# Feed-forward units past the fourth summed in one PSUM bank, scaled there by ScalarE between second and third products, with the engines' lists searched anew

## The chip, the core and the metric

The kernel runs on one core of a Trainium2 chip. The metric is the device time of one execution in microseconds (us), as the median of several runs. Inside the core, TensorE (PE, with its weight loads shown apart as PEld), VectorE (DVE), ScalarE (ACT) and GpSimd (POOL) each work through an own list of instructions in order, and wait for one another by semaphores. SyncE (SP) issues transfers. Matrix products land in PSUM, which has eight banks of 512 fp32 columns here; GpSimd has no operand in PSUM in this kernel.

## The reference

The program is an attention block with inducing points, followed by a gated feed-forward block over all tokens, in fp32. B = 4 batches of N = 12416 tokens with C = 128 channels, m = 32 inducing rows, d_ff = 1536.

```python
def mab(q, kv):
    s = scale * (q @ kv.transpose(0, 2, 1))
    s = s - s.max(-1, keepdims=True)
    a = np.exp(s)
    a /= a.sum(-1, keepdims=True) + 1e-09
    return a @ kv
h = mab(I, x)
x = mab(x, h)                      # then, on all 49664 tokens:
rms = np.sqrt(np.mean(x * x, axis=-1, keepdims=True) + 1e-06)
xn = x / rms * rms_g
g = xn @ w_gate
silu = g * (1.0 / (1.0 + np.exp(-g)))
val = xn @ w_val
out = silu * val @ w_out
```

## The kernel before

**Units and blocks.** The tokens of a batch are cut into 25 units: 20 of 512 tokens, 4 of 480 and 1 of 256, so 100 units in all (`flat`). A unit has 12 blocks (`blocks`, index j), one for each 128 of the 1536 inner columns. The 32 attention weights of a token stand for it (`a`, four stacked copies), and the gate and value weights are folded with the batch's inducing rows (`stacks`), so that a block's gate (`gate`, L720) and value (`value`, L748) are one TensorE pass each. ScalarE takes the silu (`silu`, L730), VectorE multiplies by the value (`times_value`, L762).

**Three sorts.** What follows for a block is set by its letter in the table `sorts`:

- P: `project_plain` multiplies the fp32 factor by the fp32 output weight `wo` (L818, two records in the trace for each block).
- S: the factor is left in its PSUM bank, ScalarE makes its high part (`high`, L775), VectorE the low part (`low`, L781), both as fp32r.
- D: the factor lies in SBUF, ScalarE makes the high part (L772), GpSimd the low part (`low_of_u`, L788), ScalarE scales the high part down (`high_down`, L794).

S and D then run three fp32r passes: `project_two` (L806 and L807, the first and second products), then GpSimd adds the two parts in place (`add_in_place`, L826), and `project_third` (L818) multiplies that sum by a third weight.

**Two banks a unit.** First and second products of a unit are summed in the bank `one["ups"]`; third and plain products are summed in another, `one["acc"]`. The ups sum has to be scaled by 1 + 2^-12. Four steps finish a unit: `scale_up` (E, ScalarE, L850) takes ups out of PSUM into an SBUF tile `o`, scaled and reordered; `finish` (F, VectorE, L859) adds acc to it; `turn_out` (T, VectorE, L865) transposes `o` in 32 x 32 blocks in place; `store` (O, SyncE, L880) sends it out. E needs all second products of the unit, F all third and plain ones.

**What sets the order.** There is no scheduler. The string `program` lists the steps by letter in the order in which they are issued, and each engine takes its own in that order; a dot takes the next small step of the attention of the next batch (`micros`, `taken`). Other strings give each step its resources: `banks` the PSUM bank of each product, `holders` one of 19 rooms of 512 columns for the factors (`room`), `outputs` the tile `o`, `picks` which of the waiting blocks a step takes (steps E, F, T, O take units in their order, without a pick). Rooms 0 to 8 are tiles of the pool `up`. The other ten are slices of three tiles of the first batch's x, which `rooms` opens once that batch's x has been used; the trace calls them xn.

Of the kernel before, what the change touches and what calls it, by code (L numbers as in the profile page):

```python
# [18 lines left out]
P = 128  # L19
# [4 lines left out]
def kernel(  # L24
# [40 lines left out]
    RING, HELD, SILU = 4, 9, 3  # L65
# [17 lines left out]
    psum = pool("psum", 1, space=PSUM)  # L83
    pall = psum.tile([P, 8, 512], F32, name="gv")
# [9 lines left out]
    def load_rows(b, s):  # L94

        n = per[s]
        t = xnat[b, s] = xnp.tile([P, 16 if b and n > 4 else n, C], F32, name=f"xn{s % 2 if b and n > 4 else s}")
# [592 lines left out]

    blocks, kinds = [], []
# [7 lines left out]
    def unit_of(b, u):  # L699
        if (b, u) not in at_unit:  # L700
            s, q = units[u]
            at_unit[b, u] = {"T": per2[s] * m, "a": moving.pop((b, u)), "left": NJ, "q": 0, "acc": None,
                             "k": sum(kind != "P" for kind, one in zip(kinds, blocks) if one[:2] == (b, u)), "o": None,
                             "ups": None}
# [92 lines left out]
    def project_two():  # L797
# [4 lines left out]
        if one["ups"] is None:  # L802
            one["ups"] = bank()
        to = one["ups"][:, 0:T]
# [6 lines left out]
    def project(n, lhsT, rhs, step2):  # L811
# [3 lines left out]
        if one["acc"] is None:  # L815
            one["acc"] = bank()
        to = one["acc"][:, 0:T]
        nc.tensor.matmul(to.rearrange("p (n h) -> p h n", h=2) if step2 else to, lhsT, rhs,  # L818
                         start=one["left"] == NJ, stop=one["left"] == 1)
# [18 lines left out]
    leaving = {name: 0 for name in "EFTO"}  # L838

    def next_unit(name):  # L840
        leaving[name] += 1
        return flat[leaving[name] - 1]

    def scale_up():
# [3 lines left out]
        T, o = one["T"], output(F32)  # L848
        one["o"] = o
# [11 lines left out]
    def turn_out():  # L861
        b, u = next_unit("T")
        one = unit_of(b, u)
        o, T = one["o"], one["T"]
# [393 lines left out]
    def seams():  # L1258
# [13 lines left out]
        5674130256741352764156216710562160121607267012750671527162067125701527061352701372301273016276370142374017436107  # L1272
        5461701375601735764301674317642376476324736426173214672670321071507125625625730261325620463042603435423046754672
        6571574124615247601207502765127520730717157312014520712054051402460524124361406470341720123014073145207145205162
        4076176230451603542360267402340264706402613067507602716510250673501637521352614563175416571674605740534715702545
        3457042563253265431275126142745265124560124607164701640316370347147057304132041201372013720317603270307256042750
        4756027457256347203174063021462176270675246510461307635063450634573460543604265230541265026504265026316241321643
        1064370613041320741327342735407234507234657403254130421502401325140275130732713621762170617301612506031041234610
        4621046513052135720175237120372130276215601670416415074560743514305436543215362160524062534217541646314735673157
        3561746147560274265462502530726546253601460362013460724104270371274205402507215724175061045614061306531405310463  # L1280
        5013674034130461204372104672503725074604365073047654304716046074107160721504712670235072130536725603505237062407
        2314760162062746015412574251346547516421541257642576072605210572153701357127034152342375276132436236724632174260
        7540152406524150621504361053606250125726507650216745012475627452743564527342654736024670261720742160726034704320
        1472014721542015430174301574231654215634251467354216352615236025301253012765320532154725347254712563174217637523
        0752370635767540372103120437204312072430730145703175601314341703641706327102751301341735407364103410543265123614
        2351425312634175725647256172010457015472134270321026701630513620712605763476237062046267210473623561561453612546
        3210523025043570145370641763120547163047305173501630763120750674561027475467045074507245626034013453165034150326
        4520132435743051217230723165016371043651306704754053640356435270342704175027517251427507164721453264534516342164
        5320164532405127451723407312403612753123512561726532756127032160342560324053246302542164321024052472014725041275
        4327031240370173104731643143072641362013562150613570615263174521621452643256416312654036254720764065205621562756  # L1290
        0461043103560401403507471054615042704627160734102374130415021704170527054761045260123646504615304673106351670515
        6725120513657106723017346123461762167341527647362746502364576215367425762156246276570647274635074067450367513541
        3657426517365127605360130232046352162146574051760415704761350735705327537210570673160752635725473427635274152645
        3273157425073215023576031706527106241065476140173546703573061362013651036013243162015714251640542016204310546154
        3103601765732053210642367412702173273407417520715231603573156743061471567051725417627452617425143610742642604276
        0124051264701256140
    """
    workers = """
        20120201201201020120122201201201201201211210210201020120110120120
    """  # L1300
    outputs = """
        10101010101010101010101010101010101010101010101010101010101010101010101010101010101010101010101010101010
    """
    holders = """
        abcdefghibcaedfghbicjkadelmfghnobcidepqarsfgbhidjkaeclmpnfoqrsgjhbidklaecpnfgdombrqsjihpagoecdfbknilmpghrqfsjlmc
        pkinobrsadqjhpkgfelmnoqcjrspbliadnmjkoqsglhrfejpaodnqbscriekjapmlnsqogkrbfpjhsaecokqrmdilnopgskmhqbcjrefolmnipqs
        ajdgchmkfepoirnbgqlsrpmckjfoqglnpsmibkohadprelsjmcgfnkbqolpiahdrjemsqfrcgbhnoiljepkqmrsdnloaqjifrcgpmsonblkqejrp
        hsgialnfqpojmkdsrlnqcpombeijsplqhfdagknromqepijchalskdgfbrmepqjnhgaifcokjpbrlqgeinosmdrlajpqhskmnrcfbloqmjidesag
        frklcjpqnosmhbdrlgiejkafdqpcbrmelonsfgcqjidpkhablroqenmfgicdjshaoedcinpqlgbjkhsdiorfbhgemnaqocspfjkrigbhdlmasncq
        pfedjorgbsnkclqmhefirjabposknlqemdrgibfhpoqscajnlmfhkrpecidjnbgqosljmafkdpnrqcoskihgbpefcadjlmrhosapndqkgehpjmin  # L1310
        obflrqdspkcmjnqholgaesbfkpdolhminqfjrskcpogmljdfnrqbpcaoskjhgiqmlpnefodqrmknlpcsmijknabolpshgjeidbfocgnkhqrplmjs
        oaifehgcnbdkpqclhrgfdesmjnrofkqilpgsrobkdjqlmhcnseljamrpqknfoiglspmcoqjkldhrsnpelabjmokqngircjfdhblsemqpnokjgamq
        rdlipejfmscpqonklhmgsaberjocpikmlpdsrhefqngobaljpikdmhcqsrleonfagbmpjreqolciknmpsqholfjgbakderichfsnmqopaljbrkcf
        moglhiaedbrjckqegdpsnlfrjiedkqmoaghcpsnrfblmikendagojlqhcfbmpiarsnlgckmfdhqbpoidejnaqkhipdgerbasohjlgmqienpfkrcs
        adhjnglmbpsqofekrjpidgscbljqnhepkafomgisqrnbplkcohjmfsrgkpaqbeoijdlsgnmqrfeokabpjnmlcgqhafdibeopgsrklnjcqmobkgln
        hsqdpriomajlkceshnpbofiarqsmndgejklobipnhcsgldefmraqchbjkopaslmnqirohjgdqbpmeknfsalrcidjfqokegplsdjmrknbsphcgljr
        mqasifnpeokljdhcgfrqmsolnpbekjromialsfnqpkgrjmondqlhscpnkrmbefiaojsqglkdphnmrclskoerigapjnrfbkdhlosqnmpkrsjelgpi
        acnhfjrmlpoqkdnsjbremgqkfjapdhnrifmlcesqjkbgophnrmjceoslpnadkqimofjgnbshdrlcminjoeafbkqdgpschmnjofrpdksblqamrige
        jnchpoblkqsfdagmjirnpohecqslkrpbmjdfnloqaskighmoeqcbsjrpnlagqmdikshofnejcabrlgqpdmkohirnbsldfaqjcpmkoriegsqlknjp
        ofdbshemrlqpncsgoaibklpmejshnqorkcjbplnfksqomjrdgapnqkoemicrlphjqbgnmorsfakjploqcsdnipebghorfcqksmlpjonradbcqfse  # L1320
# [240 lines left out]
```

## Time and profile before

| what | value |
| --- | --- |
| median of 3 runs | 1468.44 us (1467.72 to 1468.91) |
| the profiled execution, first to last instruction | 1467.1 us |
| mean granted TensorE clock | 0.999 |
| ScalarE busy | 1300.0 us, 89% |
| blocks of sort P, S, D | 371, 649, 180 |
| E, F, T, O steps | 100 each |
| moved by transfers | 116.02 MB, mean 79 GB/s |

The profile gives one execution, whose span is 1467.1 us. It lists each engine's busy time as the union of its records; records of one engine can overlap, so an engine's real pace is read from one start to the next. In the rows, the first name is the line of the kernel, then engine, operation, what is written and what is read.

### The profile page before, as it was taken

How to read it: one execution, taken by the hardware profiler on the slowest of the kernel's cores; microseconds unless marked ns; L12 is line 12 of the kernel's file. 1: busy time of each engine (PE TensorE's matmuls, PEld its weight loads, DVE VectorE, ACT ScalarE, POOL GpSimd, SP SyncE). 2: the span in 40 equal slices, each digit the busy share in tenths (PEclk: the TensorE clock that was granted, in tenths of full speed). 3: DMA queues.
4: the chain of work that ended last, by engine and by line, in shares of the span. 5: the costliest groups of instructions: out<-in, count | busy, mean ns of one | idle time of the engine just before them, and what ended most of it. 6: DMA issues, size and time to landing. Idle time of an engine off the chain costs nothing.

```text
span 1467.1 us, 25864 instructions
## 1 busy us (share of the span) xinstructions
PE 1460.2 (100%) x7293; PEld 1111.8 (76%) x7293; DVE 1423.3 (97%) x2476; ACT 1300.0 (89%) x2586; POOL 1353.0 (92%) x1193
## 2 busy tenths in 40 slices
PE   9999999999999999999999999999999999999998
PEld 7556777877777777786777778777778778788787
DVE  6999999999999999999999999999999999999998
ACT  6798899889988989988999899888998999899987
POOL 2578998999999999899999999799999999999998
PEclk9999999999999999999999999999999999999999
DMA  7656224445654222635554132355123111222121
GB/s 282 137 99 119 58 49 92 103 107 99 118 88 99 38 44 44 141 84 105 110 101 82 26 73 43 63 119 127 34 62 70 33 37 39 43 42 38 36 45 33
DMA packets 391904, 116.02 MB, mean 79 GB/s; under 512 B 365648, under 2 KB 371280, under 8 KB 389200
## 3 DMA queue, kind: packets, MB, share of 16 engines
q1 hardware_dynamic: 391168, 114.28, 37.7%
q8 instruction: 58, 0.95, 0.3%
q14 instruction: 86, 0.70, 0.2%
q10 hardware_dynamic: 592, 0.08, 0.0%
HBM read 53.95 MB, written 27.00 MB: 55 GB/s over the span
## 4 chain that ended last, share of the span: by engine, by line
PE 99%; DVE 0%; DMA 0%; ACT 0%; issue 0%; DVEq 0%
PE gv L818 33%; PE gv L720 17%; PE gv L748 17%; PE gv L806 12%; PE gv L807 12%; PE gv L327 3%; PE gv L380 1%; PE gv L945 1%; PE gv L574 1%; PE gv L989 0%; PE gv L468 0%; PE gv L158 0%; PE gv L490 0%; DMA ind<-in_inducing_dram 0%; PE gv L567 0%; PE gv L1099 0%
## 5 line engine op out<-in xcount | busy, mean ns | idle before, releaser
L730 ACT ACTIVATE silu<-gv 128x512 f32<-128x512 f32 (+2 forms) x1200 | 678.1, 591 | 89.4 <-PE gv L720 67.4
L826 POOL TENSOR_TENSOR xn<-xn,xn 128x512 fp32r<-128x512 f32 (+2 forms) x363 | 453.0, 1259 | 23.4 <-PE gv L807 14.5
L720 PE MATMUL gv<-a,sg 128*128 128x512 f32 (+2 forms) x1188 | 463.5, 415 | 0.1
L748 PE MATMUL gv<-a,sv 128*128 128x512 f32 (+2 forms) x1188 | 460.9, 415 | 0.0
L762 DVE TENSOR_TENSOR gv<-silu,gv 128x512 f32<-128x512 f32 (+2 forms) x649 | 427.1, 673 | 6.5 <-ACT silu L730 2.2
L775 ACT ACTIVATE xn<-gv 128x512 fp32r<-128x512 f32 (+2 forms) x602 | 353.1, 594 | 25.8 <-DVE gv L762 20.5
L818 PE MATMUL gv<-u,wo 128*128 128x512 f32 (+2 forms) x742 | 364.1, 576 | 0.0
L762 DVE TENSOR_TENSOR u<-silu,gv 128x512 f32<-128x512 f32 (+2 forms) x551 | 352.3, 654 | 7.8 <-PE gv L748 3.7
L826 POOL TENSOR_TENSOR u<-xn,u 128x512 fp32r<-128x512 f32 (+2 forms) x239 | 298.3, 1257 | 5.6 <-PE gv L807 4.1
L720 PEld LDWEIGHTS gv<-a,sg 128*128 128x128 f32 x1188 | 223.9, 189 | 86.8 <-issue 21.5
L748 PEld LDWEIGHTS gv<-a,sv 128*128 128x128 f32 x1188 | 223.8, 189 | 80.6 <-issue 23.0
L781 DVE SCALAR_TENSOR_TENSOR xn<-xn,gv 128x512 fp32r<-128x512 f32 (+2 forms) x410 | 268.9, 662 | 4.7 <-ACT xn L775 2.7
L826 POOL TENSOR_TENSOR xn<-xn 128x512 fp32r<-128x512 f32 (+2 forms) x170 | 211.4, 1250 | 11.4 <-PE gv L807 10.3
L806 PE MATMUL gv<-xn,xn 128*128 128x512 f32 (+2 forms) x450 | 177.4, 394 | 0.0
L818 PEld LDWEIGHTS gv<-u,wo 128*128 128x128 f32 x742 | 139.1, 190 | 29.7 <-issue 14.2
L788 POOL TENSOR_TENSOR xn<-u,xn 128x512 fp32r<-128x512 f32 (+2 forms) x123 | 152.3, 1243 | 6.8 <-ACT xn L772 5.5
L781 DVE SCALAR_TENSOR_TENSOR u<-xn,gv 128x512 fp32r<-128x512 f32 (+2 forms) x192 | 125.8, 660 | 1.2 <-ACT xn L775 0.9
L818 PE MATMUL gv<-xn,xn 128*128 128x512 f32 (+2 forms) x299 | 117.3, 398 | 0.0
L806 PE MATMUL gv<-xn,more 128*128 128x512 f32 (+2 forms) x302 | 116.0, 385 | 0.0
L794 ACT ACTIVATE xn<-xn 128x512 fp32r<-128x512 f32 (+2 forms) x170 | 105.6, 623 | 8.2 <-POOL xn L788 4.0
L807 PE MATMUL gv<-xn,xn 128*128 128x512 f32 (+2 forms) x299 | 111.6, 373 | 0.0
L772 ACT ACTIVATE xn<-u 128x512 fp32r<-128x512 f32 (+2 forms) x170 | 104.9, 621 | 3.9 <-DVE u L762 1.7
(233 smaller groups left out, 2049.8 us busy)
## 6 DMA issues: line engine op xcount, KB each, us to landing
out_dram<-o SPq DMA_DIRECT2D x320, 64.0 KB, 2.0
xT<-in_x_dram SPq DMA_DIRECT2D x60, 256.0 KB, 4.1
xn<-in_x_dram SPq DMA_DIRECT2D x60, 256.0 KB, 5.0
a<-hi SPq DMA_DIRECT2D x152, 64.0 KB, 2.0
a<-lo SPq DMA_DIRECT2D x152, 64.0 KB, 2.0
xn<-in_x_dram SPq DMA_DIRECT2D x5, 1024.0 KB, 9.6
xn<-w SPq DMA_DIRECT2D x18, 256.0 KB, 4.6
out_dram<-o SPq DMA_DIRECT2D x64, 60.0 KB, 2.1
```

The costliest lines, as they stand in the source:

```text
L720: nc.tensor.matmul(g[:, 0:T], stacks[b][0][:, ts(j, P)], halves_in_turn(one["a"][:, 0:T]), start=True, stop=True)
L730: nc.scalar.activation(sl[:, 0:T], gates.pop(n)[:, 0:T], AF.Silu)
L748: nc.tensor.matmul(v[:, 0:T], stacks[b][1][:, ts(j, P)], halves_in_turn(one["a"][:, 0:T]), start=True, stop=True)
L762: nc.vector.tensor_tensor(out=to, in0=sl[:, 0:T], in1=v[:, 0:T], op=ALU.mult)
L775: nc.scalar.activation(hi, t["u"], AF.Copy, scale=-(1.0 - 2.0 ** -13) * 2.0 ** -12)
L781: nc.vector.scalar_tensor_tensor(out=t["lo"], in0=t["hi"].bitcast(F32), scalar=4096.0, in1=t["u"], op0=ALU.mult, op1=ALU.add)
L788: nc.gpsimd.tensor_tensor(out=t["lo"], in0=t["u"], in1=t["hi"].bitcast(F32), op=ALU.subtract)
L794: nc.scalar.activation(t["hi"], t["hi"].bitcast(F32), AF.Copy, scale=-(2.0 ** -12))
L806: nc.tensor.matmul(to, weight_of(0, j), halves_in_turn(t["hi"]), start=not one["q"], stop=False)
L807: nc.tensor.matmul(to, weight_of(1, j), halves_in_turn(t["lo"]), start=False, stop=last)
L818: nc.tensor.matmul(to.rearrange("p (n h) -> p h n", h=2) if step2 else to, lhsT, rhs, start=one["left"] == NJ, stop=one["left"] == 1)
L826: nc.gpsimd.tensor_tensor(out=t["lo"], in0=t["hi"].bitcast(F32), in1=t["lo"].bitcast(F32), op=ALU.add)
```

## The change

Units past the fourth (`APART = 4`) use one bank for all their products. The first and second products open it; when the last second product of the unit is in, `scale_up` multiplies the bank by 1 + 2^-12 in place, PSUM to PSUM; third and plain products are then added on top without opening the bank anew. `finish` is gone for these 96 units, and `turn_out` transposes straight from the bank into a tile `o`, reading every fourth column in turn. So no third or plain product of such a unit can come ahead of its scaling. `E`, `F`, `T`, `O` now also take a pick. The ten rooms become tiles of a pool `ring`, in the place of a pool that held x of three sets.

All tables are new. `sorts` has 313 P, 753 S and 134 D (by batch, P falls from 117, 94, 88, 72 to 98, 75, 73, 67, and D goes from 49, 53, 48, 30 to 35, 41, 39, 19); `program` has 4 F.

```diff
-    RING, HELD, SILU = 4, 9, 3
+    HELD, SILU = 9, 3
+    LATE = range(full - 4, full - 1)
...
+    late = {"ctx": ctx.enter_context(ExitStack())}
+    late["x"] = late["ctx"].enter_context(tc.tile_pool(name="xlp", bufs=1))
...
+        of_set = late["x"] if not b and s in LATE else xnp
...
         kws["first"] = xnp.tile([P, half + NK, C], F32R, name=f"xn{full - 1}")
-        rings = [xnp.tile([P, RING * 512], F32R, name=f"xn{full - 4 + n}") for n in range(3)]
-        for n in range(3 * RING - 2):
-            kws[HELD + n] = rings[n // RING][:, ts(n % RING, 512)]
-        kws["last"] = rings[2][:, 2 * 512:4 * 512].rearrange("p (k c) -> p k c", c=C)
+        late["ctx"].close()
+        late["ring"] = pool("ring", 1)
+        kws["last"] = late["ring"].tile([P, 8, C], F32R, name="last")
...
-        return up.tile([P, 512], kind, name="u", tag=f"u{n}") if n < HELD else kws[n]
+        return (up if n < HELD else late["ring"]).tile([P, 512], kind, name="u", tag=f"u{n}")
...
     def project_two():
...
-        if one["ups"] is None:
-            one["ups"] = bank()
-        to = one["ups"][:, 0:T]
+        name = "ups" if one["apart"] else "acc"
+        if one[name] is None:
+            one[name] = bank()
+        to = one[name][:, 0:T]
...
     def project(n, lhsT, rhs, step2):
...
         nc.tensor.matmul(to.rearrange("p (n h) -> p h n", h=2) if step2 else to, lhsT, rhs,
-                         start=one["left"] == NJ, stop=one["left"] == 1)
+                         start=one["apart"] and one["left"] == NJ, stop=one["left"] == 1,
+                         skip_group_check=not one["apart"])
...
     def next_unit(name):
-        leaving[name] += 1
-        return flat[leaving[name] - 1]
+        return leaving[name].pop(choices.pop(0))
 
     def scale_up():
...
+        if not one["apart"]:
+            one["scaled"], to = True, one["acc"][:, 0:T]
+            nc.scalar.activation(to, to, AF.Copy, scale=1.0 + 2.0 ** -12)
+            return
+        o = one["o"] = output(F32)
...
     def turn_out():
...
+        if not one["apart"]:
+            assert not one["left"]
+            o = one["o"] = output(F32)
+            nc.vector.transpose(out=o[:, 0:T].rearrange("p (q n) -> p q n", q=R), in_=in_order(one["acc"][:, 0:T]))
+            return
+        o = one["o"]
         nc.vector.transpose(out=o[:, 0:T], in_=o[:, 0:T])
...
     sorts = """
-        PPPPPPPPPPPPPPPPPPPSPPPDPPDSPPPDPPPPPPDPDPDPSSSDPSDDDPPDPSPPDDPPPSPSSPSPSSSPPDSSDPSPPSSSSSPPDSSSSSDDSDSSPPSSSSSS
+        PPPPPPPPPPPPPPPPPPPDPPPDPPPDPPPPPPSDSDSSPDPSPSDDDPPSDSPSPSDPSSDSSPPDPSSPSPSDSSSSPPPSPDPSDSDPPSSSSPSSSPSPSSDSPSSS
```

The first place is on PE, in the third batch, where the products of that batch's unit 7 come to an end. Before (L720 gate, L748 value, L806 and L807 first and second products, L818 third or plain product; `wo` marks a plain one) its third, plain and first products alternate:

```order
L720 MATMUL gv<-a,sg 128x512 [waits DVE_49]
L818 MATMUL gv<-xn_671,xn_669 128x512
L806 MATMUL gv<-xn_671,more 128x512
L807 MATMUL gv<-xn_670,more 128x512
L748 MATMUL gv<-a,sv 128x512 [waits Activation_49]
L818 MATMUL gv<-u,wo 128x2x256 [waits DVE_49]
L720 MATMUL gv<-a,sg 128x512
L748 MATMUL gv<-a,sv 128x512 [waits Activation_49]
L806 MATMUL gv<-xn_670,xn_669 128x512
L807 MATMUL gv<-xn_670,xn_669 128x512
```

After (L724 gate, L752 value, L811 and L812 first and second products, L824 third or plain product) the unit's last first and second products stand ahead of its first third:

```order
L811 MATMUL gv<-u,more 128x512
L812 MATMUL gv<-u,more 128x512
L724 MATMUL gv<-a,sg 128x512 [waits DVE_49] x2
L724 MATMUL gv<-a,sg 128x512 [waits Activation_49]
L752 MATMUL gv<-a,sv 128x512 [waits DVE_49]
L824 MATMUL gv<-u,xn_672 128x512 [waits Activation_49,Pool_49]
L752 MATMUL gv<-a,sv 128x512 [waits DVE_49]
L824 MATMUL gv<-u,more 128x512
L824 MATMUL gv<-u,wo 128x2x256
```

Between the last second product (L812) and the first third (L824) lie four passes of the next unit. That third waits for ScalarE, whose scaling waits for L812.

The second place is on ScalarE, at the scaling of the same unit. Before (L850 the scaling, L730 silu, L775 and L794 parts of factors):

```order
L775 ACTIVATE u<-gv 128x512 [waits DVE_49]
L794 ACTIVATE xn_672<-xn_672 128x512 [waits Pool_49]
L850 ACTIVATE o<-gv 128x512 [waits DMAHW4_49,DMAHW5_49,DMAHW3_49,DMAHW2_49]
L775 ACTIVATE xn_670<-gv 128x512 [waits DVE_49,Pool_49]
L730 ACTIVATE silu<-gv 128x512 [waits PE_49]
```

After (L857 the scaling in place, L734 silu, L779 a high part, L640 a cast of the attention):

```order
L734 ACTIVATE silu<-gv 128x512 [waits PE_49,Activation_49]
L640 CAST hi<-aT 128x512 [waits DMAHW6_49,DMAHW5_49,DMAHW7_49,DMAHW4_49,DMAHW2_49]
L734 ACTIVATE silu<-gv 128x512 [waits DVE_49,PE_49]
L857 ACTIVATE gv<-gv 128x512 [waits PE_49]
L734 ACTIVATE silu<-gv 128x512 [waits DVE_49]
L779 ACTIVATE u<-gv 128x512 [waits DVE_49]
```

The scaling writes the bank that it reads. It waits for PE alone, and no longer for the store that frees a tile `o`; the turn on VectorE has that wait now.

More of the change, by code (lines that the diff above doesn't have):

```diff
@@ L96, in load_rows @@
         n = per[s]
-        t = xnat[b, s] = xnp.tile([P, 16 if b and n > 4 else n, C], F32, name=f"xn{s % 2 if b and n > 4 else s}")
+        of_set = late["x"] if not b and s in LATE else xnp
+        t = xnat[b, s] = of_set.tile([P, 16 if b and n > 4 else n, C], F32, name=f"xn{s % 2 if b and n > 4 else s}")
         if b or s == full:
@@ L689, in weight_of @@
         return kws[home_of][:, at + kind * n + j - j0, :]
+    APART = 4
     blocks, kinds = [], []
@@ L701, in unit_of @@
             s, q = units[u]
-            at_unit[b, u] = {"T": per2[s] * m, "a": moving.pop((b, u)), "left": NJ, "q": 0, "acc": None,
+            at_unit[b, u] = {"T": per2[s] * m, "a": moving.pop((b, u)), "left": NJ, "q": 0, "acc": None, "scaled": False,
                              "k": sum(kind != "P" for kind, one in zip(kinds, blocks) if one[:2] == (b, u)), "o": None,
-                             "ups": None}
+                             "ups": None, "apart": flat.index((b, u)) < APART}
         return at_unit[b, u]
@@ L816, in project @@
             one["acc"] = bank()
+        assert one["apart"] or one["scaled"]
         to = one["acc"][:, 0:T]
         nc.tensor.matmul(to.rearrange("p (n h) -> p h n", h=2) if step2 else to, lhsT, rhs,
-                         start=one["left"] == NJ, stop=one["left"] == 1)
+                         start=one["apart"] and one["left"] == NJ, stop=one["left"] == 1,
+                         skip_group_check=not one["apart"])
         one["left"] -= 1
@@ L836, in project_plain @@
         project(n, wo[:, blocks[n][2], :], u.rearrange("p (h n) -> p h n", h=2), True)
-    leaving = {name: 0 for name in "EFTO"}
+    leaving = {name: flat[:APART] if name == "F" else list(flat) for name in "EFTO"}
     def next_unit(name):
-        leaving[name] += 1
-        return flat[leaving[name] - 1]
+        return leaving[name].pop(choices.pop(0))
     def scale_up():
@@ L847, in scale_up @@
         assert one["k"] and one["q"] == one["k"]
-        T, o = one["T"], output(F32)
-        one["o"] = o
+        T = one["T"]
+        if not one["apart"]:
[3 more added lines that the diff above has]
+        o = one["o"] = output(F32)
         nc.scalar.activation(o[:, 0:T].rearrange("p (q n) -> p q n", q=R), in_order(one["ups"][:, 0:T]), AF.Copy,
@@ L863, in turn_out @@
         one = unit_of(b, u)
-        o, T = one["o"], one["T"]
+        T = one["T"]
+        if not one["apart"]:
[4 more added lines that the diff above has]
+        o = one["o"]
         nc.vector.transpose(out=o[:, 0:T], in_=o[:, 0:T])
@@ new lines @@
+        3201605123016351206531403251635032452635064736547065320476507642507614526051670146274023746120370231037437146705
+        4130675413417604510645631403561245641534306321035026310523173136017512375164731246751426754371574536741356701367
+        4053170675367153076520376157632603121563105246053213416510511643164501404716501736043703160743602376013607136314
+        2310635126502463254121562316423561275642162347635732546037260436547652563243205461024165201324052410431542301725
+        13413075103457310570135706450174650
@@ new lines @@
+        AAAAAAAGABAAAACBAADBAABBBAAAAABABAABBAAAAAAAAAABAAFAGBAAABBAAGGAAABAAACBAAAAAAABAAAAAAAAAAAAABAAAAAACACAAAAAAECD
+        AAABECACACBCAABAAAAAABAAAAAAAAABBAACBABAAADCCBAABABABDABCAABABBABAADBCBAAAAAAAAAAAACAAABBAABAABCAAABAABABCFAAEBA
+        AADBABACAAAAABAAAAABABCABAAAAAABAAABAAAAAABGECBBAAAABAAAAAAAADCBBBABAABBAAAAACAAAAAAAAAAAAABAABBAABAAAAAABHECDAA
+        AAAABACAAAAAAAAAAAAAAAAAAAABAAAAABAAABACAAABEAABABABAAAABAAAAAAABAAAABAABAAAAABAACBACAABBABABAAABBACAAAAAAAABADA
+        AAAAACAAAABABAEAAABAABADAABABAAAAA
@@ L1482 @@
+        ggqvdqsvmddhqgvpEsmdlmhTpvrrdshhrgvrqlmlsmlvgqqgvOadhsdqrpdmlmhshhggvqdddlvlgqsmlmvvrsgqvsrgmsmgvqvsmmgrsrgvEsdd
+        dmhmhlrplrgvhslqhsrdTlmgqOvqgrvmddshshgqmlldvpqrqphmlshqrOldqrgsEvprrpmddvgrmTdgrrrvpvprssmmprrpTOO
     """
     taken = """
[31 rows of a table removed]
[31 rows of a table added]
     """
```

386 lines of the change are left out of this document (189 added, 197 removed), and 62 rows, old and new, of the table taken.

## The prediction

> **What bounds the kernel now.** The page first: its row of busy times and the chain of waits.
>
> ```profile
> PE 1460.2 (100%) x7293; PEld 1111.8 (76%) x7293; DVE 1423.3 (97%) x2476; ACT 1300.0 (89%) x2586; POOL 1353.0 (92%) x1193
> PE 99%; DVE 0%; DMA 0%; ACT 0%; issue 0%; DVEq 0%
> ```
>
> TensorE is on the chain for 99% of it. A busy PE row can hide waits, because the ends of matmuls are modelled, so the second view is PE's timeline, where starts are what counts.
>
> ```profile
> 649.30 0.38 PE L806 MATMUL gv<-xn,xn 128*128 128x512 f32 x1
> 649.51 0.38 PE L807 MATMUL gv<-xn,xn 128*128 128x512 f32 x1
> 649.73 0.38 PE L720 MATMUL gv<-a,sg 128*128 128x512 f32 x1
> 649.94 0.38 PE L748 MATMUL gv<-a,sv 128*128 128x512 f32 x1
> 650.16 0.38 PE L806 MATMUL gv<-xn,xn 128*128 128x512 f32 x1
> 650.38 0.38 PE L807 MATMUL gv<-u,xn 128*128 128x512 f32 x1
> 650.59 0.38 PE L806 MATMUL gv<-xn,xn 128*128 128x512 f32 x1
> ...
> 651.24 0.38 PE L720 MATMUL gv<-a,sg 128*128 128x512 f32 x1
> ```
>
> The starts go in even steps: from 649.51 to 651.24 are eight passes, 0.216 us each, although each record says 0.38. PE really has no gaps there, so a pass taken away is worth its 0.216 us if the other engines keep up. Whether they can is in the windows (columns: PE, PEld, DVE, ACT, POOL busy):
>
> ```profile
> 0.00:30.00 30.00, 28.55 (x347) 22.88 (x351) 19.08 (x63) 16.78 (x38) 4.85 (x19) 1.00 0.78 301
> 300.00:400.00 100.00, 100.00 (x476) 73.38 (x475) 98.52 (x162) 92.25 (x194) 96.45 (x99) 1.00 0.53 100
> 600.00:700.00 100.00, 100.00 (x566) 74.92 (x565) 96.61 (x161) 89.39 (x170) 92.26 (x75) 1.00 0.51 106
> 1300.00:1400.00 100.00, 100.00 (x428) 80.29 (x427) 99.89 (x168) 92.19 (x179) 100.00 (x81) 1.00 0.20 38
> 1440.00:1467.00 27.00, 22.11 (x119) 18.99 (x117) 21.16 (x45) 17.03 (x42) 20.75 (x21) 0.96 0.22 37
> ```
>
> PE is full in all three middle windows, but VectorE stands at 97 to 100% and GpSimd at 92 to 100%. PE is the bound by a small margin, and the change must be costed on three engines.
>
> **PE: fewer plain products.** The table of sorts has 313 plain blocks (P) in place of 371. Before, they are 558 + 146 + 38 records, two a block:
>
> ```profile
> L818 PE MATMUL gv<-u,wo 128*128 128x512 f32 x558 | 282.6, 592 | 0.0
> ...
> L818 PE MATMUL gv<-u,wo 128*128 128x480 f32 x146 | 70.7, 567 | 0.0
> ...
> L818 PE MATMUL gv<-u,wo 128*128 128x256 f32 x38 | 10.8, 380 | 0.0
> ```
>
> That is 279 blocks of 512 columns, 73 of 480, 19 of 256; the new table has 236, 66 and 11. The price of a plain block again comes from starts:
>
> ```profile
> 704.23 1.02 PE L818 MATMUL gv<-u,wo 128*128 128x512 f32 x2
> 704.69 0.78 PE L720 MATMUL gv<-a,sg 128*128 128x512 f32 x1
> 705.30 0.38 PE L748 MATMUL gv<-a,sv 128*128 128x512 f32 x1
> ```
>
> From 704.23 to 705.30 lie one plain block and one gate of 0.216, so a plain block takes 0.854 us. Three products take 3 x 0.216 = 0.648. One block that changes over saves 0.206 us, less in proportion for fewer columns: 43 x 0.206 + 7 x 0.193 + 8 x 0.103 = **11.0 us**. All of it lies on the path.
>
> **VectorE.** The rows of its groups:
>
> ```profile
> L781 DVE SCALAR_TENSOR_TENSOR xn<-xn,gv 128x512 fp32r<-128x512 f32 x332 | 221.5, 675 | 3.5 <-ACT xn L775 1.6 <-POOL xn L826 0.3 <-issue 0.2
> ...
> L865 DVE STREAM_TRANSPOSE o<-o 128x512 f32<-128x512 f32 x80 | 55.9, 698 | 0.1
> L859 DVE TENSOR_TENSOR o<-gv,o 128x512 f32<-128x512 f32 x80 | 54.3, 679 | 2.6 <-PE gv L818 1.9 <-issue 0.4 <-ACT o L850 0.2
> ...
> L441 DVE STREAM_TRANSPOSE sc<-gv 128x512 f32<-128x512 f32 x19 | 12.8, 691 | 0.7 <-PE gv L327 0.6
> ```
>
> The final add (L859) goes for 96 of 100 units: 96 x 0.68 = 65 us off. Sort S rises from 649 to 753, so 104 more subtractions (L781): 104 x 0.675 = 70 us on. The turn now reads PSUM, every fourth element. Nearest rows: a turn from PSUM, unstrided, takes 691 ns (L441) against 698 from SBUF (L865); the add L859 reads PSUM in just this stride and takes 679, so neither costs by itself. I take 0, with bounds of -1 us (96 x -7 ns) and, if the stride told on turns alone by a tenth of the record, +7. Sum: **+5 us**, from +4 to +12. [...]
>
> **GpSimd and ScalarE.**
>
> ```profile
> L826 POOL TENSOR_TENSOR xn<-xn,xn 128x512 fp32r<-128x512 f32 x286 | 364.4, 1285 | 21.3 <-PE gv L807 12.9 <-DVE u L762 4.4 <-ACT xn L775 1.4
> ...
> L788 POOL TENSOR_TENSOR xn<-u,xn 128x512 fp32r<-128x512 f32 x95 | 121.4, 1283 | 5.7 <-ACT xn L772 4.8 <-ACT xn L595 0.3
> ```
>
> There are 58 more sums of two halves (L826) and, since D falls from 180 to 134, 46 fewer subtractions (L788): +58 x 1.285 - 46 x 1.283 = **+16 us**. ScalarE gets 58 more high parts at 0.60 and loses 46 scalings at about as much: +7 us, and has 167 us idle. Against spans: VectorE idles 1467.1 - 1423.3 = 43.8 us, of which 10.9 in the first 30 us and 5.8 in the last 27. With +5 and a span 11.5 us shorter some 10 us are left in between. GpSimd has 114 idle and 86 after. Both fit, VectorE only just. I take nothing for that and keep it as a rival.
>
> **The added wait.** Third and plain products of a unit now wait for the ScalarE scaling, which waits for the unit's last second product. PE runs in order: what stands behind a third product waits with it. The length of the hand-over is in the trace of before, where the scaling (L850) once waited for its last product (L807 at 649.51, above), and a ScalarE result was once waited for by VectorE:
>
> ```profile
> 649.93 0.60 ACT L850 ACTIVATE o<-gv 128x512 f32<-128x512 f32 x1 [0.33 <-PE gv L807]
> ...
> 652.21 0.59 ACT L775 ACTIVATE xn<-gv 128x512 fp32r<-128x512 f32 x1
> ...
> 652.83 0.69 DVE L781 SCALAR_TENSOR_TENSOR xn<-xn,gv 128x512 fp32r<-128x512 f32 x1 [0.45 <-ACT xn L775]
> ```
>
> That is 0.42 us to the start, 0.60 for the operation, 0.03 to the next engine: 1.05 us from the start of the last second product to the first third, if ScalarE is free. The place in PE's order shown above (third batch, unit 7) has the last second product itself and four passes of the next unit between: 5 x 0.216 = 1.08 us. So counted along the order, 94 of the 96 places have 1.04 us or more, two have 0.75 and 0.97; 32 in all have no more than 1.09, the rest 1.18 and up. So the wait is hidden, with nothing to spare at a third of the places. When ScalarE is late by part of a 0.6 us operation, PE stands for that part. In before the chain of waits shows PE behind no such hand-over, so the bounds are 0 (always on time) and, half an operation late at the 32 places, 32 x 0.3 = 10 us. I take a lateness of 0.1 us there, plus what the two short places lack: **3.5 us**. A ScalarE write into PSUM has no row here; nearest are its writes to SBUF, 0.60. [...]
>
> **The end.** The last unit loses its add:
>
> ```profile
> 1462.21 0.42 DVE L859 TENSOR_TENSOR o<-gv,o 128x256 f32<-128x256 f32 x1 [1.42 <-PE gv L818]
> 1462.67 0.45 DVE L865 STREAM_TRANSPOSE o<-o 128x256 f32<-128x256 f32 x1
> ```
>
> The turn can start 0.46 us sooner: **-0.5 us**.
>
> **Sum.** 1467.1 - 11.0 - 0.5 + 3.5 = 1459.1 us of span. The median of the runs, 1468.44, is 1.3 above the span, so **1460.4 us** (0.5% less).
>
> **Rivals.**
> *Late scaling, slower.* If ScalarE takes up the scaling late by 0.3 us at all 96 places, PE stands 29 us: 1467.1 - 11.5 + 29 + 1.3 = 1486. It undoes the gain from 0.12 us a place. For it: ScalarE is 89% busy and takes its work in order, so a scaling is on time only behind a short idle stretch like the 0.33 before 649.93. Against: it has 167 us idle, more than one such stretch a unit, and 64 of the places have 0.1 us or more to spare. Chance 0.14.
> *Full rooms, slower.* Blocks now wait for their unit, so factor rooms stay taken: counted along the program, 15.6 of 19 on average against 11.4. A late third then holds ScalarE's next high part, which holds its subtraction and later PE. If that costs PE one pass, 0.216 us, at each of the 96 units, it is 21 us: 1460.4 + 21 = 1481; it decides from 0.1 us a unit. Chance 0.05.
> *VectorE becomes the bound, no difference.* Its 10 us of idle between start and end are an average: windows such as 1300 to 1400 have none. If half of the saved PE time comes back as waits on VectorE, and the turns cost the upper 7 us, it is 1460.4 + 6 = 1466. For it: the 97 to 100% above; against: in the last batch plain blocks fall only from 72 to 67 and D from 30 to 19, so the full windows get lighter. Chance 0.13.
> *Not what it says:* the tables fix the sorts, so only the places can go wrong; no chance of its own.
>
> **How the numbers follow.** The forecast has 0.68. Its own range runs from no PE wait at all (1460.4 - 3.5, and 0.5 for the rounded starts: 1456) to the 10 us of lateness (1467). The third rival, at 1466, lies at its edge; with half of that rival's 6 us on top of the late end it reaches 1470. Above lie the two slower rivals, 0.19, and below 1456 some 0.01, so 1456 to 1470 is the range. About 0.2%, 3 us, is what a measurement of this kernel tells from no change. Faster (below 1465.5): 0.66 of the forecast's 0.68 and 0.04 of the third rival, 0.70; same: the other 0.02 and 0.08 of that rival, 0.10; slower: 0.14 + 0.05 and the last 0.01, 0.20.
>
> **What would show it.** Right: PE's group of third and plain products counts 313 x 2 plain records; its steps stay 0.216; the in-place scaling takes about 0.60 or less and PE's weight loads wait on it for under 5 us in total; the turn from PSUM stays near 0.69. Wrong: starts of third products that come regularly 0.1 us or more after the pass before; turns of 0.75 and up with VectorE at 99%; ScalarE's high parts waiting for third products.

## The result, and the profile after

| kernel | median | runs | ratio to before, 95% interval |
| --- | --- | --- | --- |
| before | 1468.26 us (1467.72 to 1468.91) | 4 | |
| changed | 1563.43 us (1562.92 to 1565.58) | 4 | 1.0651 [1.0636, 1.0666] |

The change is slower by 95 us. The forecast was 1460.4 us, with a range up to 1470, and the slowest of its rivals was put at 1486: no term and no rival had anything near 95 us. The profiled execution spans 1561.2 us, at a granted clock of 0.999, so the clock is not the reason.

The rows of the page that answer to those of before, busy times and chain of waits:

```profile
PE 1509.9 (97%) x7351; PEld 1095.3 (70%) x7351; DVE 1430.8 (92%) x2484; ACT 1308.3 (84%) x2602; POOL 1368.8 (88%) x1205
PE 85%; DVE 6%; ACT 2%; POOL 2%; issue 2%; SPq 1%; DMA 1%; DVEq 0%; POOLq 0%; ACTq 0%
```

VectorE has 7.5 us more to do than before, GpSimd 15.8, ScalarE 8.3: close to what was forecast (5, 16 and 7). Yet no engine is fuller; all of them are emptier, in share of the span. VectorE idled 43.8 us before and idles 1561.2 - 1430.8 = 130.4 us now. PE's share of the chain fell from 99% to 85%. PE's row grew by 50 us, although by the count of its products it has 11 us less to do; its records overlap (0.38 us long, 0.216 from start to start in the timeline of before), so this growth is taken as waits that the records cover, beside 51.3 us of visible gaps (6.9 before). So the time did not go into work. It went into waits, on every engine.

The groups whose prices the prediction needed, from the groups by shape:

```profile
L824 PE MATMUL gv<-u,wo 128*128 128x512 f32 x472 | 240.8, 596 | 1.3 <-POOL wo L269 1.3
...
L878 DVE STREAM_TRANSPOSE o<-gv 128x512 f32<-128x512 f32 x76 | 53.2, 701 | 0.5 <-DMA out_dram<-o 0.4
L857 ACT ACTIVATE gv<-gv 128x512 f32<-128x512 f32 x76 | 44.8, 589 | 9.7 <-PE gv L812 9.3
```

The 472 records are 236 plain blocks of 512 columns, as counted. The turn from PSUM takes 701 ns and the scaling in place 589. These prices were right. ScalarE's 8.3 us agree in part by luck: it loads its tables 30 times where it did 26 times before, at 1283 ns each in both profiles, and these 5.1 us had no term in the forecast.

Where the time was lost is in the windows (PE, PEld, DVE, ACT, POOL busy), at the places that were shown of before:

```profile
300.00:400.00 100.00, 92.99 (x458) 61.83 (x457) 86.94 (x145) 77.60 (x158) 84.61 (x77) 1.00 0.25 56
600.00:700.00 100.00, 98.11 (x581) 74.38 (x579) 90.26 (x156) 88.97 (x169) 93.38 (x78) 1.00 0.47 99
1300.00:1400.00 100.00, 99.88 (x420) 77.53 (x420) 97.96 (x162) 88.28 (x172) 97.76 (x82) 1.00 0.21 40
```

From 300 to 400 us PE has visible gaps of 7 us and VectorE stands for 13. There the attention of the next batch runs between the MLP steps. From 1300 us on there is little of it, and PE is full. What VectorE stands for is in its list of waits (total us, times, longest):

```profile
DVE sc L445 <- PE gv L331: 32.5, 21, 5.0
DVE sc L338 <- PE gv L331: 14.0, 10, 3.1
...
DVE xn L583 <- ACT silu L734: 5.6, 3, 2.6
DVE xn L583 <- PE gv L578: 4.9, 2, 2.5
```

All four are steps of the attention, none of them touched by the edit of the code: L331 makes scores on PE, L338 evicts the first scores and L445 turns the second; L578 squares, and L583 multiplies by the squares. Together they are 57 us. Before, the turn of the second scores waited 0.7 us in its main group. One place from the timeline shows what such a wait does:

```profile
346.96 0.69 DVE L482 TENSOR_TENSOR wlo<-gv,whi 96x512 fp32r<-96x512 f32 x1 [0.66 <-ACT whi L477]
...
347.84 0.59 ACT L779 ACTIVATE u<-gv 128x512 fp32r<-128x512 f32 x1
...
348.79 1.09 ACT L779 ACTIVATE u<-gv 128x512 fp32r<-128x512 f32 x2
...
352.61 0.72 DVE L445 STREAM_TRANSPOSE sc<-gv 128x512 f32<-128x512 f32 x1 [4.96 <-PE gv L331]
353.25 1.84 DVE L785 SCALAR_TENSOR_TENSOR u<-u,gv 128x512 fp32r<-128x512 f32 x3
353.38 0.48 PE L752 MATMUL gv<-a,sv 128*128 128x512 f32 x1 [0.91 <-DVE sc L445]
```

VectorE is through with L482 at 347.65. Next in its list is the turn L445, whose scores PE makes only at 351.4, so it stands for 4.96 us. Behind the turn stand three subtractions L785, whose high parts ScalarE had ready at 348.43 and 349.88. They could have run at once. They hold three banks, and PE's next value (L752) waits as well. Here one instruction that is put too early holds back everything behind it on its engine.

### The profile page after: what moved, and what is told of

Same layout as the page of the kernel before. It is cut to its first block, busy times and chain, and to the rows that moved or that the text cites. A ratio compares the mean times of both kernels' runs of the same rounds, so it can differ in the third digit from the quotient of the medians.

```text
span 1561.2 us, 26085 instructions
## 1 busy us (share of the span) xinstructions
PE 1509.9 (97%) x7351; PEld 1095.3 (70%) x7351; DVE 1430.8 (92%) x2484; ACT 1308.3 (84%) x2602; POOL 1368.8 (88%) x1205
## 4 chain that ended last, share of the span: by engine, by line
PE 85%; DVE 6%; ACT 2%; POOL 2%; issue 2%; SPq 1%; DMA 1%; DVEq 0%; POOLq 0%; ACTq 0%
PE gv L824 26%; PE gv L724 15%; PE gv L752 15%; PE gv L811 11%; PE gv L812 11%; PE gv L331 3%; DVE u L785 2%; POOL u L833 2%; DVE gv L766 1%; PE gv L384 1%; DVE u L766 1%; ACT silu L734 1%; PE gv L961 1%; ACT u L779 1%; PE gv L162 1%
## 5 line engine op out<-in xcount | busy, mean ns | idle before, releaser
L833 POOL TENSOR_TENSOR u<-u 128x512 fp32r<-128x512 f32 (+2 forms) x887 | 1083.0, 1252 | 71.1 <-PE gv L812 59.9
L734 ACT ACTIVATE silu<-gv 128x512 f32<-128x512 f32 (+2 forms) x1200 | 678.9, 592 | 110.6 <-PE gv L724 62.1
L766 DVE TENSOR_TENSOR gv<-silu,gv 128x512 f32<-128x512 f32 (+2 forms) x753 | 488.2, 670 | 14.5 <-ACT silu L734 8.0
L785 DVE SCALAR_TENSOR_TENSOR u<-u,gv 128x512 fp32r<-128x512 f32 (+2 forms) x753 | 481.4, 659 | 13.1 <-ACT u L779 7.5
L779 ACT ACTIVATE u<-gv 128x512 fp32r<-128x512 f32 (+2 forms) x753 | 431.2, 595 | 64.4 <-DVE gv L766 53.5
L724 PE MATMUL gv<-a,sg 128*128 128x512 f32 (+2 forms) x1188 | 461.6, 413 | 15.8 <-DVE sc L338 3.9
L752 PE MATMUL gv<-a,sv 128*128 128x512 f32 (+2 forms) x1188 | 458.6, 412 | 14.4 <-DVE u L766 3.1
L824 PE MATMUL gv<-u,wo 128*128 128x512 f32 (+2 forms) x626 | 310.9, 583 | 1.3 <-POOL wo L269 1.3
L724 PEld LDWEIGHTS gv<-a,sg 128*128 128x128 f32 x1188 | 223.1, 189 | 121.9 <-DVE u L785 20.3
L752 PEld LDWEIGHTS gv<-a,sv 128*128 128x128 f32 x1188 | 223.5, 189 | 112.4 <-issue 23.4
L766 DVE TENSOR_TENSOR u<-silu,gv 128x512 f32<-128x512 f32 (+2 forms) x447 | 286.5, 655 | 11.4 <-PE gv L752 2.8
L792 POOL TENSOR_TENSOR u<-u 128x512 fp32r<-128x512 f32 (+2 forms) x134 | 167.1, 1251 | 41.0 <-ACT u L776 29.5
L811 PE MATMUL gv<-u,more 128*128 128x512 f32 (+2 forms) x390 | 154.3, 396 | 1.5 <-ACT u L798 0.7
L824 PE MATMUL gv<-u,more 128*128 128x512 f32 (+2 forms) x390 | 151.0, 403 | 1.9 <-POOL rs L612 1.8
L812 PE MATMUL gv<-u,more 128*128 128x512 f32 (+2 forms) x390 | 146.2, 375 | 2.0 <-DVE u L785 1.9
L824 PEld LDWEIGHTS gv<-u,wo 128*128 128x128 f32 x626 | 116.1, 190 | 29.1 <-issue 13.8
L811 PE MATMUL gv<-u,xn 128*128 128x512 f32 (+2 forms) x338 | 134.1, 397 | 1.1 <-DVE u L766 0.6
L824 PE MATMUL gv<-u,xn 128*128 128x512 f32 (+2 forms) x338 | 134.1, 410 | 0.5 <-ACT gv L857 0.2
L812 PE MATMUL gv<-u,xn 128*128 128x512 f32 (+2 forms) x338 | 126.8, 375 | 1.1 <-DVE u L785 1.1
L776 ACT ACTIVATE u<-u 128x512 fp32r<-128x512 f32 (+2 forms) x134 | 83.4, 627 | 11.3 <-DVE u L766 10.8
L811 PEld LDWEIGHTS gv<-u,more 128*128 128x128 f32 x390 | 73.8, 189 | 26.6 <-issue 8.0
L824 PEld LDWEIGHTS gv<-u,more 128*128 128x128 f32 x390 | 73.3, 189 | 25.1 <-issue 13.7
```

Source lines behind the costliest of these rows:

```text
L724: nc.tensor.matmul(g[:, 0:T], stacks[b][0][:, ts(j, P)], halves_in_turn(one["a"][:, 0:T]), start=True, stop=True)
L734: nc.scalar.activation(sl[:, 0:T], gates.pop(n)[:, 0:T], AF.Silu)
L752: nc.tensor.matmul(v[:, 0:T], stacks[b][1][:, ts(j, P)], halves_in_turn(one["a"][:, 0:T]), start=True, stop=True)
L766: nc.vector.tensor_tensor(out=to, in0=sl[:, 0:T], in1=v[:, 0:T], op=ALU.mult)
L776: nc.scalar.activation(hi, t["u"], AF.Copy, scale=1.0 - 2.0 ** -13)
L779: nc.scalar.activation(hi, t["u"], AF.Copy, scale=-(1.0 - 2.0 ** -13) * 2.0 ** -12)
```

## The experiments

Three theories went into the runs. A: the new lists set the attention's steps too close to what they wait for. B: the wait for the scaling costs directly. C: rooms and banks are held longer, or the pools cost something. The changed kernel is at 1563.4 and before at 1467.9 to 1468.6 beside them.

**1. The new code with the old tables.**

```diff
-    APART = 4
+    APART = 100
...  (and the tables of before; each E, F, T, O takes the first unit)
```

> The new functions with the tables of before: APART is 100, so every unit keeps two banks, its scaling into o and its final add; the ten late rooms are tiles of the new pool. Nothing of the new order is left. Theory A (the new lists set the attention's products on PE and their readers on VectorE too close, and VectorE stands there) and theory B (the wait for the scaling costs directly) both expect the time of before, 1468 us within 3. Theory C (the rooms as tiles of a pool of their own, or the moved x tiles, add waits) expects 1475 or more.

Measured: 1468.38 us, ratio 1.0000 [0.9991, 1.0009]. Pools, moved tiles and picks cost nothing; the loss lies in the use of one bank or in the tables.

**2. The changed kernel without its scaling.**

```diff
-            one["scaled"], to = True, one["acc"][:, 0:T]
-            nc.scalar.activation(to, to, AF.Copy, scale=1.0 + 2.0 ** -12)
+            one["scaled"] = True
```

> The changed kernel without the in-place scaling of the 96 units: ScalarE does nothing there and no third or plain product waits for it; the order of all else stays. It leaves out the factor 1 + 2^-12. Theory B expects most of the 95 us back, 1470 to 1490. Theory A expects the waits for the scaling alone to go, which in the trace of the changed kernel are 11 us of late thirds at most and 45 us of ScalarE's own work off an engine that is no bound: 1550 to 1563. Theory C expects 1560.

Measured: 1559.74 us, ratio 1.0623 [1.0607, 1.0638]. With the wait and the operation both gone, 3.7 us come back. As a direct cost theory B has fallen.

**3 and 4. VectorE's readers of attention products made free, in both kernels.**

```diff
-            nc.vector.transpose(out=sc[b][rows2[s], cols2[s]], in_=st.pop(("s2", s)))
+            rows = st.pop(("s2", s)).shape
+            nc.vector.transpose(out=sc[b][rows2[s], cols2[s]], in_=xT[b, s][0:rows[0], 0:rows[1]])
...  (the eviction L338 likewise; L583 becomes a transpose of its SBUF tile in place)
```

> The changed kernel with its order, but VectorE's three readers of attention products (the evictions of the first scores, the turns of the second scores, the products with the squares) are transposes of a tile in SBUF of the same size, so they wait for no product of PE; the products are still made. It leaves out the attention's numbers. Theory A: VectorE stood 32.5 + 14.0 us for the scores and 10.5 before the products with the squares, 57 us; if PE's lost time comes from there, 40 to 57 of the 95 us come back: 1506 to 1523. Theories B and C expect 1555 to 1563, since neither the scaling nor the rooms are touched.

> The same edit on the kernel before, as a control. Theory A: its VectorE waited about 1 us in all for these products, so nothing is to be won: 1465 to 1475. If instead the edit itself makes VectorE faster or takes load off, it would come out below 1460 and the gain in the run beside it would prove nothing.

Measured: 1515.62 us for the changed kernel, ratio 1.0323 [1.0306, 1.0340]; 1477.09 for the one before, ratio 1.0060 [1.0045, 1.0075]. The changed kernel gets 47.8 us back; the old one gets nothing and pays 9.1 for the edit, 2 us above what was expected. The edit cuts the tie on both sides: PE no longer waits for these readers either before it writes their banks again. VectorE's list of waits in the third run no longer has these steps ahead; its longest totals are others:

```profile
DVE gv L770 <- ACT silu L738: 11.3, 10, 3.7
DVE u L789 <- ACT u L783: 9.5, 34, 0.8
```

So half of the loss is shown to hang on the tie between PE and three kinds of readers in VectorE's list.

**5 and 6. The attention of batches 1 to 3 cut out of both kernels' lists.** What is left is the MLP in each kernel's order.

> The kernel before with all attention steps of batches 1 to 3 taken out of the lists: the MLP steps, their order, banks and rooms stay. It leaves out those batches' attention; their units read a tile of x and the weights of batch 0. All theories: shorter than 1468, since 64 us of PE's and 140 us of VectorE's work are gone; the lists, made for the attention in between, may give back only a part, 1430 to 1460. It is the yardstick for the run beside it.

> The same cut in the changed kernel. Theory A (the loss comes from where the attention's steps stand): with them gone the changed MLP steps are no slower than those of the run beside it, from 11 us faster (the plain passes saved) to 5 slower. Theories B (the wait for the scaling) and C (rooms and banks held longer) lie in the MLP steps themselves and expect a difference of 50 to 95 us to stay.

Measured: 1453.28 us (ratio 0.9898 [0.9884, 0.9913]) and 1464.06 us (0.9970 [0.9958, 0.9982]). The difference between the forms is 10.8 us where it was 95. So 84 of the 95 us are there only while the attention stands in the lists. This cut takes away the attention's place in the lists and its load together (VectorE's row falls by 125.5 us, from 1423.3 to 1297.8, in the kernel before), so it does not tell the two apart; runs 9 and 10 do. The clocks differ a little as well: 0.994 in run 5, 0.999 in run 6. In run 5 PE's two longest waits are 4.7 and 3.9 us, and its granted clock is 0.98 from 300 to 500 us and from 500 to 700, where run 6 has 1.00 and 0.99. By an estimate from the two means, 0.005 of 1452 us, that is worth 7 us at most, so at one clock the difference would be 11 to 18 us and the attention's share 77 to 84. The difference that is left missed the expectation, which ended at 5 slower. The first 100 us hold part of it, as the windows show, of the cut kernel before and of the cut changed one:

```profile
0.00:100.00 100.00, 98.30 (x683) 64.79 (x684) 83.94 (x185) 74.98 (x157) 46.15 (x67) 1.00 0.39 136
```

```profile
0.00:100.00 100.00, 91.69 (x655) 57.84 (x656) 80.63 (x178) 67.43 (x146) 42.13 (x60) 1.00 0.36 128
```

PE has 6.6 us more of gaps there, where weights are still being prepared and only the first units have begun. The lists put those steps otherwise too. The full kernels show the same there: PE busy 98.2 us of the first 100 before, 91.7 changed, so some 6.5 of the 95 us are lost at the start, and the prediction had no term for that either.

**7. The wait for the scaling without the attention.** Run 6 with the edit of run 2.

> The changed kernel cut to its MLP steps in batches 1 to 3, as before, and without the in-place scaling (the factor 1 + 2^-12 is left out): what the wait for the scaling costs where no attention is in the way. If it is what makes the cut change 11 us slower than the cut old form, 1450 to 1456; if it is as small as in the full kernel (4 us), 1459 to 1463.

Measured: 1458.24 us, ratio 0.9933 [0.9918, 0.9948]: 5.8 us less than run 6, between the two expectations. The scaling, wait and operation together, is about half of the 10.8.

**8. Attention steps moved, on all engines.** The tables `program`, `taken` and `picks` made anew; MLP steps keep their order on each engine.

> The changed kernel, complete, with each engine's MLP steps in the order of the changed lists and with the same banks and rooms; only attention steps stand elsewhere among them: PE's products earlier or their readers later, as far as banks and tiles allow (34 loads of ScalarE's tables where the changed kernel has 30 and before 26). Theory A: VectorE's 57 us of waits shrink by about half, 20 to 35 us come back: 1528 to 1543. Theories B and C: 1558 to 1570.

Measured: 1589.59 us, ratio 1.0828 [1.0810, 1.0847]. Slower, against theory A's numbers. VectorE's waits for the second scores did fall, to 6.9 us. But SP's transfers had been moved with the rest: PE's list of waits has a new head, and SP's queue (SPq) stands in the chain of waits:

```profile
PE gv L724 <- DMA a<-lo: 23.2, 2, 16.5
PE 83%; DVE 5%; ACT 3%; SPq 3%; issue 2%; POOL 2%; DMA 1%; DVEq 0%; ACTq 0%; POOLq 0%
```

Twice PE waited for a unit's tile `a`, once 16.5 us, since on SP's queue the transfers that fill it had come behind loads of x. The 3% of SP's queue are about 48 us; the next run has 0% there. The granted clock is lower too: 0.986 over the whole run against 0.999 in the changed kernel, by an estimate from these two worth 22 us at most. On its page the clock is at 8 tenths in two slices, from 357.0 to 436.4 us, and at 9 in the other 38; in the first of the two PE is busy for 6 tenths, its emptiest slice. The run moved too much to speak against theory A.

**9. The same with SP's and ScalarE's order kept.**

> As the run with the attention moved, but SP's and ScalarE's queues keep the order of the changed lists (30 table loads, as there); only on PE, VectorE and GpSimd do attention steps stand elsewhere among the MLP steps, whose own order, banks and rooms stay. Complete. Theory A: without the late gathers of the run before it (PE waited 23 us for tiles a behind x loads on SP's queue), a good half of VectorE's 57 us of waits and what hangs on them comes back: 1520 to 1540. Theories B and C: 1558 to 1570.

Measured: 1529.86 us, ratio 1.0421 [1.0405, 1.0436], with nothing of the computation left out: 33.6 us come back without touching an operation, the order of any MLP step on its engine, or anything in SP's and ScalarE's lists. VectorE's wait for the second scores, 32.5 us in the changed kernel:

```profile
DVE sc L445 <- PE gv L331: 3.8, 4, 1.8
```

**10 and 11. All lists made anew, with the scaling and without it.** For these, a rule walked through the steps with the durations of the records: each engine takes a step that can start within a short time, the earlier one in the old list where several can. SP keeps its order. Small shifts of priority were tried for the shortest span by those durations.

> The changed kernel, complete, with the same steps and the same sorts (313 P, 753 S, 134 D), but new lists: on each engine but SP, whose order stays, the next step is one that can start within 0.15 us, the earlier one of the changed lists where several can, by the durations of the records; banks and rooms are given out anew, the longest free first. Theory A: most of the 95 us is the order of the lists and nothing in the operations: 1468 to 1500. Theory B: every unit still waits for its scaling, so 1540 or more. Theory C: the rooms are as many and held as long, so 1540 or more.

> The relisted kernel without the in-place scaling (it leaves out the factor 1 + 2^-12), all else in its order. What the scaling costs where the order is not in the way. Theory A: 2 to 6 us less than the run beside it. Theory B: 20 us less or more.

Measured: 1507.43 us (ratio 1.0269 [1.0252, 1.0286]) and 1504.49 us (1.0248 [1.0232, 1.0263]). With the same operations and sorts, 56 of the 95 us come from the lists alone. This misses theory A's range, which ended at 1500, by 7 us, and is far below what B and C expected. The scaling costs 2.9 us here. VectorE is fuller than in the changed kernel (95% of the span, 92% there), and PE's visible gaps fall from 51 to 20 us:

```profile
PE 1485.6 (99%) x7351; PEld 1099.5 (73%) x7351; DVE 1432.9 (95%) x2484; ACT 1306.1 (87%) x2602; POOL 1367.1 (91%) x1205
```

**12. The old form, with lists made by the same rule.** Needed to read run 10 rightly.

> The form of before (two banks for every unit, 371 P, 649 S, 180 D) with lists made anew in the same way as those of the relisted kernel. It is the yardstick for it: what new lists alone are worth without the change. Theory A1 (the changed form is good, its lists are bad): near 1468, within 5, since PE has no gap there to close but at the start and the end. Theory A2 (the changed form itself leaves the lists less room, for every third and plain product stands behind its unit's scaling): the old form takes new lists well, 1455 to 1468, and stays 35 us or more below the relisted change.

Measured: 1484.37 us, ratio 1.0112 [1.0096, 1.0129]. Both expectations missed: the rule makes lists that are 16 us worse than the old ones. So run 10's distance to before is partly the rule's own. By the same rule the changed form is 1507.4 - 1484.4 = 23 us slower than the old one. Taken with one set of lists for each form, the 95 us fall into three parts: 56 that new lists win for the changed form, 16 that they lose for the old one, and 23 that stay between the forms.

**13. A second set of lists for the changed form, less tight.**

> The changed form with another set of lists, made as the first but with 0.09 us more allowed for every hand-over between engines, so that steps are not put as close. If the 39 us that are left in the relisted kernel are hand-overs put too close, 1480 to 1500; if they lie in what the changed form asks of any list, 1500 to 1515.

Measured: 1519.56 us, ratio 1.0348 [1.0332, 1.0363]. Steps set further apart did not help, and the time lies above both expectations. The two sets of lists differ by 12 us, which tells how much one set of lists by this rule can move.

**14. The changed form with fewer S blocks, lists by the same rule.**

> The changed form with 58 of its S blocks, evenly spread, made plain again (371 P, 695 S, 134 D), and lists made anew in the same way as the first relisted kernel. PE has its 11 us of plain passes back, GpSimd has 58 sums and VectorE 58 subtractions fewer. If the 23 us by which the relisted change stays above the relisted old form come from the load that the new sorts put on VectorE and GpSimd, 1484 to 1495. If they come from the form itself or from the list-making, the load counts for nothing and PE's passes come on top: 1505 to 1518.

Measured: 1510.73 us, ratio 1.0292 [1.0275, 1.0309]. GpSimd has 68 us less to do than in run 10 and VectorE 26, as the rows of busy times say, and nothing is won:

```profile
PE 1488.3 (99%) x7293; PEld 1094.8 (73%) x7293; DVE 1407.3 (93%) x2426; ACT 1284.4 (85%) x2544; POOL 1299.0 (86%) x1147
```

So the load of the new sorts is unlikely to be what keeps the changed form above the old one; 12 to 23 us were expected for it. It is not excluded, since one set of lists can differ from another by 12 us.

**What stays open.** Why the changed form needs 23 us more than the old one under lists of one rule. The direct wait for the scaling is 3 to 6 us of it. That blocks are held longer, because they stand behind their unit's scaling, and so leave every list less freedom, fits but was not shown: more rooms were not tried, and a rule that walks from the changed lists may find worse lists for the form than there are. A further rival was not tested. The rule left SP's order alone, so run 10 has the transfers in the order of the changed lists and run 12 in that of the old ones. In the first 100 us PE is busy for 93.3 us in run 10 and 97.8 in run 12, and the DMA engines' busy share is 0.47 and 0.68; the 101st product of the gate's line (L724) starts at 179.4 us and 172.2. So some 7 of the 23 us are there before the second batch, and whether the transfers' order makes them is open. No complete version here beats the kernel before.

## Why the prediction was wrong, point by point

- **Plain passes, -11.0 us.** The count was right. The saving is work off PE, but it cannot be seen in the total: PE stood for other engines for longer than it saved. Run 14, which gives PE those passes back, is 3.3 us slower than run 10, within the 12 us by which two sets of lists differ; so no run here shows the saving by itself.
- **VectorE +5, GpSimd +16, ScalarE +7.** Measured 7.5, 15.8 and 8.3, the last in part by luck (the four table loads). The turn from PSUM at no extra cost was right: 701 ns against 698 from SBUF. So was the "about 0.60 or less" for the scaling in place: it took 589 ns for 128x512, and the scaling to SBUF 604 in the kernel before.
- **The added wait, 3.5 us.** Runs 2, 11 and 7 measured 3.7, 2.9 and 5.8. These runs leave out the wait and the operation together, so they bear out the size and not the working behind it (0.1 us late at 32 places). In the changed kernel's trace PE and its weight loads wait for the scaling 16 times, 4.6 us in all, under the 5 us that the prediction named as a sign of being right. The rival "late scaling" (29 us of waits) did not happen.
- **The step that failed** is "Both fit, VectorE only just", with "worth its 0.216 us if the other engines keep up" ahead of it. It set sums of busy time against the span, and so took the order of the new lists as free. But all tables were new, and the prediction priced a moved instruction at one place only, the end of a unit. The attention's steps had been moved too, on five engines, and had no term at all. Sums say whether an engine could keep up; whether it does depends on what stands ahead in its list. The missing term, which the prediction put at nothing, is 34 us by run 9, where attention steps alone moved on three engines, and 56 by run 10, where all lists but SP's were made anew; runs 5 and 6 put what hangs on the attention, place and load, at 77 to 84.
- **"VectorE becomes the bound"** named the right engine by the wrong mechanism: VectorE did not fill up, it stood. How little a stall on VectorE could be hidden was in the profile of before: 27 us of idle between start and end, some 10 after the forecast's own terms, against the 57 us of waits that the new list brings it.
- **"Full rooms"** was priced at 21 us. Run 14 takes load away and wins nothing, which neither shows nor excludes it.
- **What would have shown it beforehand:** the two orders lay open. For each attention product on PE, the steps behind it on VectorE up to its reader could have been counted against those on PE, as was done for the scaling. That count was not made here either, so how much of the 95 us it would have given is not known.

## What to carry to other kernels

When a change comes with new order tables, the tables can be the larger part of the change, as they were here: price each kind of hand-over between engines whose two ends moved, not only those that the code edit names. On this kernel, where three engines are over 90% busy, spare time in the sums bought nothing for an instruction that stands at the head of its queue too early. And a rebuilt order has to be compared with the old form under lists made the same way, or the list-maker's own loss is read as the change's.

## What the runs showed of the hardware that was not expected

- VectorE's 32 x 32 transpose of 128x512 fp32 took 701 ns from PSUM with a stride of four elements (L878, changed), and 698 from SBUF to SBUF (L865, before).
- With the attention of batches 1 to 3 gone, 1453 us are left of 1468 in the old lists: these lists held their time although 125.5 us of VectorE's work were taken out.
- Run 8, where PE waited once for 16.5 us, has a granted clock of 0.986, against 0.999 in the changed kernel. Its clock is at 8 tenths from 357.0 to 436.4 us, where PE is busy for 6 and 8 tenths; that the gap made it so was not shown.
- With attention steps moved on SP's and ScalarE's lists as well, the kernel takes 1589.6 us, against 1529.9 with those two lists kept. SP's queue is on the chain for about 48 us in the first and for none in the second, so most of the 60 us is likely the order of the transfers. ScalarE's list was put back at the same time, and part is the lower clock, so the share of each was not shown.
